# Second matrix of a sparse-attention and feed-forward kernel in two scaled halves, with a rewritten opening

## The chip, the cores and the metric

One core of one Trainium2 chip runs the whole program. The metric is device microseconds (us) of one execution. The engines are TensorE (PE, and PEld for its weight loads), VectorE (DVE), ScalarE (ACT), GpSimd (POOL) and SyncE (SP); SP and POOL also issue the DMA transfers that matter here, each on a queue of its own.

## The reference

Attention in blocks of 32 over 768 positions, then a feed-forward layer on its output. Only the parts that set the shapes are kept:

```python
B, H, S, D = 4, 8, 768, 64           # float32 q, k, v
mask = np.abs(blk_i - blk_j) <= 1
mask = mask | (blk_i == 0) | (blk_j == 0) | (blk_i == n_blocks - 1) | (blk_j == n_blocks - 1)
for qb in range(n_blocks):           # 24 blocks, 3 random ones for each
    for kb in sampled_blocks[qb]:
        mask[qb*32:(qb+1)*32, kb*32:(kb+1)*32] = True
scores = np.where(mask, q @ k.T / np.sqrt(D), -1e9)
attn = np.exp(scores - scores.max(-1, keepdims=True))
attn = attn / (attn.sum(-1, keepdims=True) + 1e-9)
x = (attn @ v).transpose(0, 2, 1, 3).reshape(3072, 512)
h = x @ w_in                          # 512 x 2048, float64
g = h * erf(np.maximum(h, 0) + np.log1p(np.exp(-np.abs(h))))
return g @ w_out                      # 2048 x 512, float64; out float32
```

## The kernel before, in words

**Numbers.** Products of the feed-forward layer and of the values run in f16: each factor is scaled by a power of two and split into a high half and a low half, and three of the four products of halves are added. The scale comes from a bound, the root of a sum of squares: `bound`, `whole_sum` and `pow2_scale` (L200) reduce the squares on each partition, add them over the partitions with one small matmul, and build the scale and its inverse with a few one-column steps on VectorE. The matrices arrive as 64-bit floats. For a pair of row blocks k (0 to 7) of `w_in` (i) or `w_out` (o) the program has five steps, named by a letter, the matrix and the pair: D decodes the raw words in three VectorE passes (`decode_pair`, L464), Q squares on ScalarE, H makes the high half on ScalarE, L the low half on VectorE; A and B (`sum_w`, `scale_w`) make the matrix' scale once all eight pairs are squared. Before, `w_out` has one scale, so no half of it exists before its eighth square.

**Attention.** A batch has three chunks of two tiles of four query blocks. A unit is a tile's scores for half of the heads (two pairs of heads): scores, maximum (`soft_max`), exponential on ScalarE (`soft_exp`), high and low half of the probabilities (`soft_low`), turning (`soft_turn`). Keys of the random blocks are copied by GpSimd. The values are split into four parts, `split_v` (L257), written to a table in DRAM (`vtab`), and gathered from there into `vb` by block number, the numbers being read from `samp` by `TENSOR_LOAD`. `values_of` multiplies, `norm` divides, `turn` splits and transposes the result for the feed-forward layer.

**Order.** Every instruction is kept in program order on its engine by the helper `InOrder`, so all rows of the trace carry its line, L59. The opening (L875 to L971) is written out by hand: loads, the bound of v, units 0 to 3, the decodes of `w_in` between them, its halves. Then a loop (L978) of 98 steps m runs over 96 groups of 256 rows of the feed-forward layer (4 batches, 3 chunks, 8 groups): the first product (`ff_first`) of group m, the gate of group m-1 (`ff_gate`, L726), the second product (`ff_second`, L735) of group m-2, and one attention unit in most steps. What is left of the two matrices' steps hangs in three tables of the loop, EARLY, AMID and LATE (L27 to L38), by step m: EARLY stands after `norm`, AMID after the gate's exponential, LATE after the turned probabilities.

```python
        if m < len(EARLY):
            work(EARLY[m])
        if m >= FF_LAG:
            for u in range(CT):
                ff_second(*groups[m - FF_LAG], u)
        if unit:
            soft_max(unit)
```

The accumulators `o` of a chunk take all eight groups, then `ff_store` (L748) multiplies by `iso` and writes. The raw words of the matrices are loaded by `load_weight`: 16 loads of 512 KB for each, on SP's or GpSimd's queue; those of `w_out` start as the decodes of `w_in` free their places (L472).

Of the kernel before, what the change touches and what calls it, by code (L numbers as in the profile page):

```python
# [18 lines left out]
P = 128  # L19
# [23 lines left out]
def sparse_attention_moe(ctx: ExitStack, tc: tile.TileContext, qT, kT, v, sampled, w_in, w_out, out):  # L43
# [140 lines left out]

    one = cp.tile([P, 1], F32, tag="one", name="one")
# [14 lines left out]
    def pow2_scale(whole, tag):  # L200
# [5 lines left out]
        s = st.tile([P, 1], F32, tag="s_" + tag[:2], name=f"s_{tag}", bufs=1)  # L206
        inv = st.tile([P, 1], F32, tag="i_" + tag[:2], name=f"i_{tag}", bufs=1)
# [43 lines left out]
    vns = {}  # L251

    def place_v(b, quad, half):

        place, tag, bufs = (mo, "xT", 3) if b == 0 and (quad, half) < (1, 1) else (at, "vn", 1)
        vn = place.tile([P, KT, 2, VW], F16, tag=tag, name=f"vn_{b}_{quad}_{half}", bufs=bufs)
        pool.memset(vn[:, :, :, D : D + 2], 1.0)  # L257
        vns[b, quad, half] = vn

    def split_v(b, quad, half):  # L260

        s = vscale[b][0]
# [9 lines left out]
        write = (whole_rows(b)[:, :, c : c + 2 * VW], vn.rearrange("p k h c -> p k (h c)"))  # L272
        if b == 0:
            sp.dma_start(*write)
        else:
            writes.append(write)
# [38 lines left out]
    kgs = {}  # L315
    POOL, SYNC = mybir.EngineType.Pool, mybir.EngineType.SP
# [13 lines left out]
    def gather(b, t):  # L330

        first, last = 1 + 4 * t, min(5 + 4 * t, NB - 1)
        blocks = block_numbers(first, last, POOL)
# [79 lines left out]
    wo16 = wo.rearrange("p n c -> p (n c)").bitcast(F16).rearrange("p (n c) -> p n c", c=1024)  # L413
    wsq = {"i": sums[:, P : P + 8], "o": sums[:, P + 8 : P + 16]}
# [49 lines left out]
    def decode_pair(key, k):  # L464
# [19 lines left out]
    def sum_w(key):  # L484
        wsums[key] = bound(wsq[key], f"w{key}", ALU.add)

    def scale_w(key):
        wscale[key] = pow2_scale(whole_sum(wsums.pop(key), f"w{key}"), f"w{key}")

# [245 lines left out]
    def ff_second(b, ch, fg, u):  # L735
        if fg == 0:
# [3 lines left out]
        for j in range(FG):  # L740
# [24 lines left out]

    results = []
# [118 lines left out]
    for n in range(3):  # L885
        place_v(0, *divmod(n, 2))
# [4 lines left out]
    for pr in range(HP):  # L891
        order_k(0, pr)
    place_v(0, 1, 1)
    order_q(0, 0)
    have_k.add(0)
    gathers(0)
# [15 lines left out]
    work("Di0")
    soft_low(units[0])
    work("Qi0")
    have_v.add(0)

# [157 lines left out]
```

## Time and profile before

| | |
|---|---|
| time, median of 3 runs | 838.31 us (838.24 to 840.38) |
| span of the profiled execution | 836.8 us |
| TensorE busy | 710.8 us, 85% of the span |
| VectorE busy | 554.4 us, 66% |
| ScalarE busy | 601.1 us, 72% |
| GpSimd busy | 123.7 us, 15% |
| DMA, mean | 157 GB/s |

The span is that of one execution taken by the hardware profiler; the page gives no other time for it, and it is set beside the median of the runs. Busy shares are averages over the span: an engine with 85% may be full in one stretch and starved in another. The stretch up to the first matmuls of the loop (87 us) and the first dozen steps of the loop are where the lines of the diff act; the gates of all later steps are touched as well.

### The profile page before, as it was taken

How to read it: one execution, taken by the hardware profiler on the slowest of the kernel's cores; microseconds unless marked ns; L12 is line 12 of the kernel's file. 1: busy time of each engine (PE TensorE's matmuls, PEld its weight loads, DVE VectorE, ACT ScalarE, POOL GpSimd, SP SyncE). 2: the span in 40 equal slices, each digit the busy share in tenths (PEclk: the TensorE clock that was granted, in tenths of full speed). 3: DMA queues.
4: the chain of work that ended last, by engine and by line, in shares of the span. 5: the costliest groups of instructions: out<-in, count | busy, mean ns of one | idle time of the engine just before them, and what ended most of it. 6: DMA issues, size and time to landing. Idle time of an engine off the chain costs nothing.

```text
span 836.8 us, 26712 instructions
## 1 busy us (share of the span) xinstructions
PE 710.8 (85%) x11100; PEld 504.8 (60%) x11100; DVE 554.4 (66%) x977; ACT 601.1 (72%) x999; POOL 123.7 (15%) x344
## 2 busy tenths in 40 slices
PE   1253637899897899899999899999999899999997
PEld 1252424566665667566777666667777576766664
DVE  3994796887764766766566676756677567654454
ACT  4654657987865766887768778868678678776774
POOL 5430111001222220100201231000111100000000
PEclk9775867989998999999999999999999999999999
DMA  8999953687899697661497886633576758211000
GB/s 325 297 257 318 243 120 90 164 207 164 172 212 209 178 205 198 186 131 45 136 216 178 210 198 192 167 79 83 117 167 166 190 103 188 53 33 40 1 27 26
DMA packets 199930, 131.61 MB, mean 157 GB/s; under 512 B 144000, under 2 KB 167168, under 8 KB 199808
## 3 DMA queue, kind: packets, MB, share of 16 engines
q1 hardware_dynamic: 196384, 118.10, 58.1%
q0 software_dynamic: 3424, 11.80, 4.3%
q8 instruction: 87, 1.43, 0.7%
q14 instruction: 35, 0.29, 0.1%
HBM read 83.88 MB, written 12.95 MB: 116 GB/s over the span
## 4 chain that ended last, share of the span: by engine, by line
PE 47%; DVE 15%; issue 12%; ACT 10%; DMA 10%; SPq 2%; POOL 2%; POOLq 1%; ACTq 0%
PE h L59 18%; PE o L59 18%; PE s_m L59 5%; DMA vb<-vtab 4%; PE po L59 3%; DVE g L59 2%; ACT pf_m L59 2%; DVE q L59 2%; DVE mx_m L59 2%; DMA vtab<-vn 2%; SPq L59 2%; ACT x L59 2%; DVE p_m L59 2%; POOL kg L59 2%; ACT q L59 2%
## 5 line engine op out<-in xcount | busy, mean ns | idle before, releaser
L59 PE MATMUL h<-xT,wi 128*128 128x256 f16 x2304 | 274.2, 276 | 14.9 <-ACT wi L59 7.5
L59 PE MATMUL o<-wo,g 128*128 128x512 f16 x1152 | 270.3, 385 | 7.9 <-DVE wo L59 4.0
L59 PEld LDWEIGHTS <-wi 128*128 128x128 f16 x2304 | 227.4, 99 | 65.5 <-ACT wi L59 8.8
L59 PEld LDWEIGHTS <-g 128*128 128x128 f16 x1152 | 110.3, 99 | 133.0 <-issue 14.8
L59 ACT ACTIVATE x<-x 128x512 f32<-128x512 f32 x288 | 181.5, 630 | 9.1
L59 POOL COPY kg<-kx 128x128 f32 x264 | 90.5, 394 | 286.2 <-PE s_m L59 183.6
L59 ACT ACTIVATE pf_m<-s_m,nb_m 128x256 f32<-128x256 f32 x160 | 62.7, 475 | 65.4 <-DVE nb_m L59 59.5
L59 DVE SCALAR_TENSOR_TENSOR q<-x,q 128x512 f32<-128x512 f32 x96 | 66.7, 695 | 61.4 <-ACT x L59 60.1
L59 ACT ACTIVATE x<-h,isg 128x512 f32<-128x512 f32 x96 | 65.2, 680 | 36.3 <-PE h L59 35.7
L59 PE MATMUL s_m<-kx,qm 128*64 128x64 f32 (+1 forms) x1280 | 75.0, 249 | 6.8 <-ACT pf_m L59 4.2
L59 ACT ACTIVATE q<-q 128x512 f32<-128x512 f32 x96 | 59.5, 620 | 29.6 <-DVE q L59 29.6
L59 DVE SCALAR_TENSOR_TENSOR q<-q,h 128x512 f32<-128x512 f32 x96 | 65.5, 682 | 22.6 <-ACT q L59 22.6
L59 DVE TENSOR_TENSOR p_m<-pf_m,p_m 128x1024 f16<-128x1024 f32 x40 | 49.3, 1232 | 32.3 <-ACT p_m L59 32.3
L59 DVE SCALAR_TENSOR_TENSOR g<-q,g 128x512 f16<-128x512 f32 x96 | 67.0, 698 | 3.3
L59 PE MATMUL po<-vb,pT_m 128*32 128x65 f16 (+1 forms) x3840 | 44.7, 201 | 25.7 <-DMA vb<-vtab 15.0
L59 PEld LDWEIGHTS s_m<-kx,qm 128*64 128x64 f32 x1280 | 59.7, 146 | 10.4 <-ACT pf_m L59 4.9
L59 ACT ACTIVATE q<-x 128x512 f32<-128x512 f32 x96 | 60.5, 630 | 3.1
L59 DVE TENSOR_REDUCE mx_m<-s_m 128x4 f32<-128x1024 f32 x40 | 48.8, 1219 | 20.2 <-PE s_m L59 20.2
L59 PEld LDWEIGHTS <-pT_m 128*32 128x32 f16 x3840 | 38.0, 97 | 36.8 <-DMA vb<-vtab 16.3
L59 PE MATMUL s_m<-kg,qm 128*64 128x96 f32 x640 | 46.9, 261 | 3.2 <-POOL kg L59 2.2
L59 DVE TENSOR_TENSOR x<-xf,x 128x512 f16<-128x512 f32 x24 | 16.9, 703 | 43.3 <-ACT x L59 43.3
L59 DVE TENSOR_SCALAR g<-q 128x512 f16<-128x512 f32 x96 | 41.3, 431 | 3.3
(115 smaller groups left out, 623.7 us busy)
## 6 DMA issues: line engine op xcount, KB each, us to landing
vb<-vtab SPq DMA_DIRECT2D x280, 65.0 KB, 2.9
vb<-vtab SPq DMA_DIRECT2D x32, 390.0 KB, 4.1
vraw<-in_v_dram SPq DMA_DIRECT2D x10, 768.0 KB, 5.1
vtab<-vn SPq DMA_DIRECT2D x16, 390.0 KB, 5.4
vb<-vtab SPq DMA_DIRECT2D x12, 520.0 KB, 5.0
qt<-in_qT_dram SPq DMA_DIRECT2D x20, 256.0 KB, 3.3
out_dram<-wo SPq DMA_DIRECT2D x20, 256.0 KB, 4.3
vb<-vtab SPq DMA_DIRECT2D x36, 130.0 KB, 3.0
```

Of the source, the lines that this page charges most:

```text
L59: done = call(*args, **kwargs)
```

## The change

Three things are done together.

1. `w_out` has two scales, one for pairs 0 to 3 (key p) and one for pairs 4 to 7 (key q), kept in a tile `levels`. The first chunk's second product uses both: its accumulators are closed after four groups, scaled by the inverse of p's scale into `partial`, opened again for the other four, and added at the end. A new step C (`level`) takes the smaller of the two scales for all later chunks, and a share for each half by which the gate (`ff_gate`) is multiplied: from a column of `levels` instead of a constant, in 88 of the 96 gates.
2. The opening loads v ahead of k and q, puts all four parts of v's halves in one place (`first_v`, in `wo`), writes them in two transfers instead of four, reads the first block numbers early, and copies the last two pairs of keys on GpSimd instead of VectorE. Raw blocks 0 to 5 of `w_in` are loaded by SP, the others by GpSimd, 8 to 15 behind gathers; raw blocks 0 to 7 of `w_out` are loaded by SP behind the eighth decode, behind the gathers of the values so far.
3. The opening and the tables are rewritten: four halves of `w_in` are made ahead of the loop, one decode of `w_out`; in the loop the high halves of `w_out` from pair 5 on stand in AMID of the step whose LATE has their low half (before: high in LATE of one step, low in AMID of the next).

```diff
-EARLY = ("", "", "Ao Bo Ho0 Lo0", "Hi5", "Hi6", "Hi7")
-AMID = ("Do3 Qo1 Qo2", "Do5", "", "Li5 Lo2", "Li6 Lo3", "Li7 Lo4", "Lo5", "Lo6", "Lo7")
+EARLY = ("Do1", "Ap Bp Ho0", "", "", "", "Aq", "Lo4")
+AMID = ("Qo0 Qo1 Do2", "Lo0 Do4", "Do5", "Ho2 Do6", "Ho3 Do7", "Hi7", "Ho5", "Ho6", "Ho7")
 LATE = (
-    "Qo3 Do4 Hi2 Li2 Qo4 Hi3 Li3",
-    "Qo5 Do6 Qo6 Do7 Qo7",
-    "Hi4 Ho1 Li4 Lo1 Ho2",
-    "Ho3",
-    "Ho4",
-    "Ho5",
-    "Ho6",
-    "Ho7",
+    "Qo2 Do3 Qo3",
+    "Ho1 Qo4 Lo1 Wo12 Wo13 Wo14 Wo15",
+    "Hi4 Qo5 Li4",
+    "Lo2 Hi5 Qo6 Li5",
+    "Lo3 Hi6 Qo7 Li6",
+    "Li7 Bq Cq Ho4",
+    "Lo5",
+    "Lo6",
+    "Lo7",
 )
...
-        copy = pool.tensor_copy if b else dve.tensor_copy if pr > 1 else act.copy
+        copy = pool.tensor_copy if b or pr > 1 else act.copy
...
         if b == 0:
-            sp.dma_start(*write)
+            if half == 1:
+                four = first_v[:, :, quad * 4 : quad * 4 + 4].rearrange("p k h c -> p k (h c)")
+                sp.dma_start(whole_rows(b)[:, :, quad * QW : quad * QW + QW], four)
...
+    first_v = wo[:, 11:, :].rearrange("p n c -> p (n c)").bitcast(F16)[:, : KT * H * VW]
...
-        freed = {4: (0, 1), 5: (2, 3), 6: (4, 5), 7: (6, 7)} if key == "i" else {2: (8, 9), 3: (10, 11)}
+        freed = {} if key == "i" else {2: (8, 9), 3: (10, 11)}
         for i in freed.get(k, ()):
-            load_weight(sp if key == "i" and k > 4 else pool, "o", i)
+            load_weight(pool, "o", i)
...
+        parts = wsq["i"] if key == "i" else wsq["o"][:, :4] if key == "p" else wsq["o"][:, 4:]
+        wsums[key] = bound(parts, f"w{key}", ALU.add)
...
+    def level(key):
+        (sp_, ip), (sq_, iq) = wscale["p"], wscale["q"]
+        least = levels[:, 4:5]
+        dve.tensor_tensor(least, sp_, sq_, ALU.min)
+        whole = levels[:, 5:6]
+        dve.tensor_tensor(whole, ip, iq, ALU.max)
+        wscale["o"] = (least, whole)
+        for c, n, inv in ((6, "p", ip), (7, "q", iq)):
+            shares[n] = levels[:, c : c + 1]
+            dve.tensor_scalar(shares[n], least, inv, 2.0**-H_SHIFT, ALU.mult, ALU.mult)
...
     def ff_gate(b, ch, fg):
-        scale = 2.0**-H_SHIFT
+        scale = 2.0**-H_SHIFT if (b, ch) == (0, 0) else shares["p" if fg < NGR // 2 else "q"]
         dve.scalar_tensor_tensor(hs, hs, -1.0, h, ALU.add, ALU.mult)
         dve.tensor_scalar(g[:, 0], hs, scale, None, ALU.mult)
...
     def ff_store(b, ch, fg, u):
+        early = (b, ch) == (0, 0)
+        if fg == NGR - 1 or (early and fg == NGR // 2 - 1):
+            key = "o" if not early else "p" if fg < NGR // 2 else "q"
...
+            ob = partial[0][:, u] if key == "p" else wo[:, NF + t % 2, :]
+            if key == "q":
+                dve.scalar_tensor_tensor(ob, outs[u], iso, partial[0][:, u], ALU.mult, ALU.add)
+            elif u == 0:
                 act.activation(ob, outs[u], AF.Copy, scale=iso)
             else:
                 dve.tensor_scalar(ob, outs[u], iso, None, ALU.mult)
...
+    for quad in range(2):
+        load_v(0, quad)
     for pr in range(HP):
         load_k(0, pr)
     load_q(0, 0)
-    for quad in range(2):
-        load_v(0, quad)
-    for i in range(4):
+    for i in range(6):
         load_weight(sp, "i", i)
-    load_q(0, 1)
-    load_q(0, 2)
...
-    work("Qi6 Di7 Qi7 Do0")
-    set_apart()
+    work("Qi6 Di7 Qi7")
+    for i in range(8):
+        load_weight(sp, "o", i)
...
-    work("Bi")
+    work("Bi Hi0")
     first_scale(0)
     values_of(seen(units[1]))
+    norm(*seen(units[1]))
     gathers(0)
-    for i in (12, 13, 14, 15):
-        load_weight(pool, "o", i)
-    norm(*seen(units[1]))
-    work("Hi0")
+    set_apart()
+    work("Li0 Hi1")
     turn(*seen(units[1]))
...
-    work("Li0 Hi1")
-    soft_turn(units[3])
     norm(*seen(units[2]))
-    work("Li1 Do1")
     values_of(seen(units[3]))
-    work("Qo0")
     norm(*seen(units[3]))
+    work("Li2 Hi3")
     turn(*seen(units[3]))
-    work("Do2")
+    work("Li3 Do0")
     gathers(0)
```

SP's queue at the start of the program, where `vb<-in_v_dram` and `vraw` are the two loads of v, `kr` those of k, `qt` of q, `wi` raw blocks, `vtab` the writes of v's halves and `vb<-vtab` gathers. Before:

```order
L59 DMA samp_85<-in_sampled_dram 128x144
L59 DMA kr_0_106<-in_kT_dram 128x768
L59 DMA qt_0_114<-in_qT_dram 128x4x128
L59 DMA vb<-in_v_dram 128x4x384
L59 DMA vraw_1_117<-in_v_dram 128x1536
L59 DMA wi<-in_w_in_dram 128x1024 x4
L59 DMA qt_1_123<-in_qT_dram 128x4x128
L59 DMA qt_2_125<-in_qT_dram 128x4x128
L320 TENSOR_LOAD samp
L59 DMA vtab_94<-vn_0_0_127 128x6x260
L59 DMA vtab_94<-vn_0_1_129 128x6x260
```

And with the change:

```order
L60 DMA samp_85<-in_sampled_dram 128x144
L60 DMA vb<-in_v_dram 128x4x384
L60 DMA vraw_1_108<-in_v_dram 128x1536
L60 DMA kr_0_110<-in_kT_dram 128x768
L60 DMA qt_0_118<-in_qT_dram 128x4x128
L60 DMA wi<-in_w_in_dram 128x1024 x6
L325 TENSOR_LOAD samp
L60 DMA vtab_95<-wo 128x6x520 x2
L60 DMA qt_1_254<-in_qT_dram 128x4x128
L60 DMA qt_2_256<-in_qT_dram 128x4x128
L60 DMA vb<-vtab_95 32x2x1040 x2
```

Both loads of v now stand ahead of the keys, two more weight loads stand ahead of the writes, the later q loads behind them, and two writes take the place of four.

VectorE at the end of the opening, where `rinv`, `xf` and `x` belong to `norm` and `turn`, `wi<-wi,s_wi` is a low half of `w_in`, and three passes from `wo` by `spare_k` back to `wo` are one decode of `w_out`. Before:

```order
L59 SCALAR_TENSOR_TENSOR wi<-wi,s_wi 128x2x512
L59 TENSOR_SCALAR spare_k<-wo 128x1024
L59 SCALAR_TENSOR_TENSOR spare_k<-wo,spare_k 128x1024
L59 SCALAR_TENSOR_TENSOR wo<-wo,spare_k 128x1024
L59 TENSOR_SCALAR rinv_1_1_1206<-po_1_1_1107 128x4
L59 RECIPROCAL rinv_1_1_1206<-rinv_1_1_1206 128x4
L59 TENSOR_TENSOR xf_1_1101<-po_1_1_1107,rinv_1_1_1206 128x256
L59 TENSOR_TENSOR x_0_1_1210<-xf_1_1101,x_0_1_1210 128x512
L59 TENSOR_SCALAR spare_k<-wo 128x1024
L59 SCALAR_TENSOR_TENSOR spare_k<-wo,spare_k 128x1024
L59 SCALAR_TENSOR_TENSOR wo<-wo,spare_k 128x1024
L59 TENSOR_REDUCE mx_m_2_0_1326<-s_m_2_0_1301 128x4
```

And with the change:

```order
L60 TENSOR_SCALAR rinv_1_1_1187<-po_1_1_1090 128x4
L60 TENSOR_TENSOR xf_1_1088<-po_1_1_1090,rinv_1_1_1187 128x256
L60 SCALAR_TENSOR_TENSOR wi<-wi,s_wi 128x2x512
L60 TENSOR_TENSOR x_0_1_1193<-xf_1_1088,x_0_1_1193 128x512
L60 SCALAR_TENSOR_TENSOR wi<-wi,s_wi 128x2x512
L60 TENSOR_SCALAR spare_k<-wo 128x1024
L60 SCALAR_TENSOR_TENSOR spare_k<-wo,spare_k 128x1024
L60 SCALAR_TENSOR_TENSOR wo<-wo,spare_k 128x1024
L60 TENSOR_SCALAR spare_k<-wo 128x1024
L60 SCALAR_TENSOR_TENSOR spare_k<-wo,spare_k 128x1024
L60 SCALAR_TENSOR_TENSOR wo<-wo,spare_k 128x1024
L60 TENSOR_REDUCE mx_m_2_0_1311<-s_m_2_0_1283 128x4
```

Before, the second decode stands ahead of the last values' division (`rinv_1_1`) and the third ahead of unit 4's maximum (`mx_m_2_0`). Now two low halves of `w_in` stand around `x`, then the first decode, the last work of the opening, and the second one, that of EARLY[0].

VectorE in m6, where `mx_f` and `nb_f` are the unit's maximum, `q_0_6` and `g` belong to the gate, `p_f` is the low half of its probabilities, `wo<-wo,...` is a low half of `w_out`, and `vn` the low halves of the next values. Before:

```order
L59 TENSOR_REDUCE mx_f_0_2623<-s_f_0_2599 128x1
L59 TENSOR_SCALAR nb_f_0_2625<-mx_f_0_2623 128x1
L59 SCALAR_TENSOR_TENSOR q_0_6_2478<-x_0_6_2474,q_0_6_2478 128x512
L59 SCALAR_TENSOR_TENSOR wo<-wo,s_wo 128x2x512
L59 TENSOR_TENSOR p_f_0_2630<-pf_f_0_2628,p_f_0_2630 128x768
L59 SCALAR_TENSOR_TENSOR vn_1_1_2641<-vraw_1_1964,s_v_2438,vn_1_1_2641 128x6x64 x2
```

And with the change:

```order
L60 SCALAR_TENSOR_TENSOR wo<-wo,levels 128x2x512
L60 TENSOR_REDUCE mx_f_0_2635<-s_f_0_2608 128x1
L60 TENSOR_SCALAR nb_f_0_2637<-mx_f_0_2635 128x1
L60 SCALAR_TENSOR_TENSOR q_0_6_2487<-x_0_6_2483,q_0_6_2487 128x512
L60 TENSOR_TENSOR p_f_0_2642<-pf_f_0_2640,p_f_0_2642 128x768
L60 SCALAR_TENSOR_TENSOR wo<-wo,levels 128x2x512
L60 SCALAR_TENSOR_TENSOR vn_1_1_2653<-vraw_1_1948,s_v_2447,vn_1_1_2653 128x6x64 x2
```

There is one low half more in this step (pair 4's, ahead of the maximum), and pair 5's now stands behind `p_f` instead of ahead of it.

## Rows read from the trace of the kernel before

**Rows 1.** The page: span, and busy time of the engines with share and instructions.

```profile
span 836.8 us, 26712 instructions
...
PE 710.8 (85%) x11100; PEld 504.8 (60%) x11100; DVE 554.4 (66%) x977; ACT 601.1 (72%) x999; POOL 123.7 (15%) x344
```

**Rows 2.** Table of stretches: stretch, length, busy PE, PEld, DVE, ACT, POOL, granted clock, DMA, GB/s.

```profile
16.80:60.00 43.20, 20.67 (x338) 18.40 (x338) 40.71 (x50) 27.73 (x48) 17.50 (x31) 0.76 0.98 290
60.00:87.24 27.24, 9.18 (x322) 6.93 (x323) 14.53 (x30) 12.10 (x17) 4.40 (x14) 0.62 0.98 296
87.24:134.50 47.26, 25.48 (x326) 17.00 (x326) 35.58 (x51) 30.08 (x51) 7.47 (x16) 0.72 0.56 145
134.50:175.05 40.55, 34.08 (x674) 24.30 (x673) 34.17 (x59) 36.64 (x59) 4.84 (x19) 0.91 0.75 184
87.24:91.60 4.36, 4.36 (x26) 3.06 (x27) 1.32 (x2) 0.00 (x0) 1.05 (x2) 0.62 0.87 207
176.30:203.73 27.43, 25.44 (x453) 18.24 (x451) 20.76 (x36) 21.35 (x34) 4.03 (x8) 1.00 0.83 180
```

**Rows 3.** Timeline, 57 to 130 us: start, duration, engine, work, [idle before it, releaser].

```profile
59.74 1.22 DVE L59 TENSOR_REDUCE mx_m<-s_m 128x4 f32<-128x1024 f32 x1
...
77.87 0.16 DVE L59 TENSOR_SCALAR rinv<-po 128x4 f32<-128x4 f32 x1 [9.32 <-PE po L59]
...
87.24 4.36 PE L59 MATMUL h<-xT,wi 128*128 128x256 f16 x24 [1.11 <-ACT xT L59]
```

**Rows 4.** Timeline of TensorE, 80 to 260 us.

```profile
125.64 0.59 PE L59 MATMUL whole_wo<-one,top_wo 128*128 128x1 f32 x2 [11.62 <-DVE top_wo L59]
...
128.54 0.59 PE L59 MATMUL o<-wo,g 128*128 128x512 f16 x1 [2.31 <-ACT wo L59]
...
176.30 2.78 PE L59 MATMUL h<-xT,wi 128*128 128x256 f16 x24
...
203.73 0.39 PE L59 MATMUL s_e<-kx,qm 128*64 128x96 f32 x4 [1.99 <-ACT pf_f L59]
```

**Rows 5.** Timeline, the start.

```profile
6.62 1.95 ACT L59 COPY kx<-kr 128x768 f32<-128x768 f32 x4 [4.58 <-DMA kr<-in_kT_dram]
...
11.19 0.86 DVE L59 COPY qm<-qt 64x512 f32<-64x512 f32 x2 [0.16 <-DMA qt<-in_qT_dram]
...
13.06 0.84 ACT L59 ACTIVATE vj<-vb 128x768 bf16<-128x768 f32 x1 [4.49 <-DMA vb<-in_v_dram]
...
16.83 0.16 DVE L59 TENSOR_REDUCE top_v<-vsq 128x1 f32<-128x4 f32 x1 [4.78 <-ACT vj L59]
```

**Rows 6.** Groups of VectorE by form: out<-in, count | busy us, mean ns | idle before.

```profile
L59 DVE SCALAR_TENSOR_TENSOR g<-q,g 128x512 f16<-128x512 f32 x96 | 67.0, 698 | 3.3
...
L59 DVE TENSOR_SCALAR g<-q 128x512 f16<-128x512 f32 x96 | 41.3, 431 | 3.3
...
L59 DVE SCALAR_TENSOR_TENSOR spare_k<-wo,spare_k 128x1024 int32<-128x1024 int32 x10 | 12.3, 1226 | 0.3
...
L59 DVE SCALAR_TENSOR_TENSOR wo<-wo,s_wo 128x1024 f16<-128x1024 f32 x8 | 10.2, 1280 | 1.7 <-ACT wo L59 1.7
L59 DVE TENSOR_SCALAR wo<-o,iso 128x512 f32<-128x512 f32 x12 | 9.0, 751 | 3.7 <-PE o L59 2.8
...
L59 DVE TENSOR_SCALAR spare_k<-wo 128x1024 int32<-128x1024 int32 x10 | 7.0, 701 | 0.1
```

**Rows 7.** Chain of waits, 0 to 100 us: start, duration, what.

```profile
24.96 12.14 DMA vtab<-vn
...
71.40 4.59 DMA vb<-vtab
```

**Rows 8.** DMA view, 34 to 76 us: queue, packets, MB, share of 16 engines.

```profile
q0 software_dynamic: 1728, 6.29, 48.6%
```

**Rows 9.** Chain that ended last, whole span, by line.

```profile
by line: PE h L59 18.4%; PE o L59 18.2%; issue 11.9%; PE s_m L59 4.8%; DMA vb<-vtab 3.8%; PE po L59 3.3%; DVE g L59 2.4%; ACT pf_m L59 2.3%; DVE q L59 2.2%; DVE mx_m L59 2.1%; DMA vtab<-vn 2.0%; SPq L59 2.0%; ACT x L59 2.0%; DVE p_m L59 1.8
```

**Rows 10.** DMA view, 0 to 130 us: GB/s in 40 slices of 3.25 us.

```profile
GB/s 23 285 388 418 413 384 404 388 335 252 134 249 371 300 325 276 276 168 204 189 358 310 241 327 406 340 216 189 310 222 183 339 226 102 85 0 233 170 0 0
```

More of the change, by code (lines that the diff above doesn't have):

```diff
@@ L332, in gather @@
         first, last = 1 + 4 * t, min(5 + 4 * t, NB - 1)
-        blocks = block_numbers(first, last, POOL)
+        blocks = first_numbers.pop() if first_numbers else block_numbers(first, last, POOL)
         for i in range(first, last):
@@ L484, in sum_w, with scale_of @@
     def sum_w(key):
-        wsums[key] = bound(wsq[key], f"w{key}", ALU.add)
+        parts = wsq["i"] if key == "i" else wsq["o"][:, :4] if key == "p" else wsq["o"][:, 4:]
+        wsums[key] = bound(parts, f"w{key}", ALU.add)
     def scale_w(key):
         wscale[key] = pow2_scale(whole_sum(wsums.pop(key), f"w{key}"), f"w{key}")
+    def scale_of(key, k):
+        return wscale[key if key == "i" else "p" if k < 4 else "q"][0]
     def halves(key, k):
@@ L495, in split_hi @@
         w32, hi16, _ = halves(key, k)
-        act.activation(hi16, w32, AF.Copy, scale=wscale[key][0])
+        act.activation(hi16, w32, AF.Copy, scale=scale_of(key, k))
     def split_lo(key, k):
         w32, hi16, lo16 = halves(key, k)
-        dve.scalar_tensor_tensor(lo16, w32, wscale[key][0], hi16, ALU.mult, ALU.subtract)
-    steps_of = {"D": decode_pair, "Q": square_pair, "A": sum_w, "B": scale_w, "H": split_hi, "L": split_lo}
+        dve.scalar_tensor_tensor(lo16, w32, scale_of(key, k), hi16, ALU.mult, ALU.subtract)
+    shares = {}
+    def level(key):
[8 more added lines that the diff above has]
+            dve.tensor_scalar(shares[n], least, inv, 2.0**-H_SHIFT, ALU.mult, ALU.mult)
+    steps_of = {
+        "D": decode_pair,
+        "Q": square_pair,
+        "A": sum_w,
+        "B": scale_w,
+        "H": split_hi,
+        "L": split_lo,
+        "C": level,
+        "W": lambda key, k: load_weight(pool, key, k),
+    }
     def work(steps):
@@ L735, in ff_second @@
     def ff_second(b, ch, fg, u):
-        if fg == 0:
+        turns = (0, NGR // 2) if (b, ch) == (0, 0) else (0,)
+        starts = [n * FG for n in turns]
+        stops = [n - 1 for n in starts[1:]] + [NF - 1]
+        if fg in turns:
             outs[u] = ps_o.tile([P, DM], F32, tag="o", name=f"o_{b}_{ch}_{fg}_{u}")
@@ L757, in ff_store @@
                 dve.tensor_scalar(ob, outs[u], iso, None, ALU.mult)
+            if key == "p":
+                return
             r = b * S
@@ L890, in sparse_attention_moe @@
     dve.tensor_scalar(unity, column, pidx, None, ALU.is_equal)
[L891 to L896, printed above, removed]
+    first_numbers.append(block_numbers(1, 5, POOL))
     numbers[0] = block_numbers(1, 5, SYNC)
     early.append((0, 1))
-    for i in range(4, 10):
-        load_weight(pool, "i", i)
     for quad in range(2):
@@ L904, in sparse_attention_moe @@
     scale_v(0)
+    order_k(0, 0)
+    split_v(0, 0, 0)
+    order_k(0, 1)
+    order_k(0, 2)
+    order_k(0, 3)
+    split_v(0, 0, 1)
+    for i in (6, 7):
+        load_weight(pool, "i", i)
+    split_v(0, 1, 0)
+    order_q(0, 0)
+    split_v(0, 1, 1)
+    load_q(0, 1)
+    load_q(0, 2)
+    have_k.add(0)
+    have_v.add(0)
+    gathers(0)
+    for i in range(8, 12):
+        load_weight(pool, "i", i)
+    work("Di0")
     scores(units[0])
-    split_v(0, 0, 0)
-    split_v(0, 0, 1)
+    work("Qi0 Di1")
     soft_max(units[0])
-    split_v(0, 1, 0)
-    split_v(0, 1, 1)
     soft_exp(units[0])
[L912 to L915, printed above, removed]
+    work("Qi1 Di2")
     scores(units[1])
@@ L919, in sparse_attention_moe @@
     gathers(0)
-    for i in range(10, 16):
+    for i in range(12, 16):
         load_weight(pool, "i", i)
+    soft_low(units[0])
     soft_turn(units[0])
-    work("Di1")
+    work("Qi2 Di3")
     soft_max(units[1])
@@ L926, in sparse_attention_moe @@
     order_q(0, 1)
-    work("Qi1 Di2 Qi2 Di3 Qi3")
+    work("Qi3 Di4")
     soft_low(units[1])
+    scores(units[2])
     soft_turn(units[1])
-    scores(units[2])
-    work("Di4 Qi4 Di5")
+    work("Qi4 Di5")
     soft_max(units[2])
```

47 lines of the change are left out of this document (26 added, 21 removed).

## The prediction

> **What bounds the kernel now.** I read four views in this order. The page gives the share of each engine: TensorE is busy for 85% of the span, VectorE for 66%, ScalarE for 72% [rows 1]. An average says little here, so the table of stretches comes next: up to 60 us VectorE works almost without a hole (40.71 of 43.20 us), from 60 to 175 us it has holes, and TensorE falls behind in the whole stretch to 134.5 us [rows 2]. Two timelines then show the stalls that this change is about: the second tile's values wait for gathered rows (VectorE, which needs them next, waits 9.32 us), and TensorE waits 11.62 us ahead of the common scale of the second matrix [rows 3, 4]. From 176.30 us on TensorE runs without a gap that matters until 203.73 us (25.44 of 27.43 us busy, granted clock 1.00) [rows 2, 4]. So time is to be won only before 175 us, and what is won there must still be there when TensorE fills up.
>
> I call a pass over one half of the second matrix' pairs "half p" (pairs 0 to 3) and "half q" (4 to 7), and m0, m1, ... the steps of the main loop; m0's first matmul is at 87.24 us [rows 3].
>
> **The ledger.** VectorE ends last in most of this stretch, and up to the reduction of the loop's m6, which ends at the edge of a stretch in the table (175.05 us), it does the same work before and after. So I count: start, work, idle time. Before, it starts with the bound of v at 16.83 us [rows 5]; to 175.05 it is busy for 40.71 + 14.53 + 35.58 + 34.17 = 125.0 us of 158.2 and idle for 33.2: 2.5, 12.7, 11.7 and 6.4 by stretch [rows 2].
>
> *Start.* Four key loads and q stood ahead of v. Now v is first: its first load lands about when the first key load did (6.62 us, plus up to 1 us as it is twice as large) and no longer at 13.06; the squares took from there to 16.83, 3.77 us [rows 5]. Now they end at 11.3 to 12.4; I take 11.8, 5.0 us earlier.
>
> *Work added.* A second scale (a reduction and four steps of about 0.16 us, as the reduction in rows 5), four such steps for the least common level, and the eviction of half p's sum for one tile at 0.75 us [rows 6] with its 0.16 us factor: 2.5 us. The copy of q, 0.86 us [rows 5], moves behind the start. Together 3.4 us. The two key copies go from VectorE to GpSimd, where the gathers wait for ScalarE's copy of the second pair anyway: nothing; without that cover, their own copy time once, ahead of the first scores.
>
> *Gathers.* The two larger writes are issued after eight halves: the last was issued at 24.96 us [rows 7], now 5 us earlier, about 20. That write took 12.14 us and the last gather landed at 71.40 + 4.59 = 75.99 [rows 7], 38.9 us after the write. In that stretch GpSimd's queue moved 6.29 MB, twelve loads of 512 KB, at 48.6% of 42 us, so 1.70 us of all engines each [rows 8]. The change leaves four of the twelve there (the last four of the first matrix): 38.9 - 8 x 1.70 = 25.3 us. The write lands between 32 us (12.14 after its issue) and 39 (the third rival); I take 33, since its queue holds two more weight loads. The last gather then lands at 58. It is needed when unit 3 has been turned, at about 68 (below), so the 9.32 us wait is gone, with 10 us of cover. The eight raw loads of the second matrix that follow on SP's queue are needed 18 us later and have the queues to themselves.
>
> *Idle time to m0.* Of 2.5 + 12.7 us, 9.3 go: 5.9 stay. But a hole needs work to fill it: the second and third decode of the second matrix, three passes of 0.70, 1.23 and about 1.23 us each, so 6.3 us [rows 6], stood there and now stand behind m0's matmuls. I add 6: 12 us in all. The first matmul of m0 follows. Behind the last half of v at 20 us stand eight first-matrix decodes (25.3), four reductions of 1.22 us [rows 3] with a 0.16 us step each (5.5), three low halves of probabilities (3.6, an estimate: each like a decode's second pass) and 2.5 us of holes: unit 3's reduction ends at 56.9 instead of 61.0 [rows 3]. From there to 87.24 were 26.2 us; less 9.3 for the gathers, and 2.6 more for two added low halves of the first matrix (1.28 each, as those of the second [rows 6]): m0 begins at about 76, 11 us earlier.
>
> *Idle time m0 to m2.* The 11.7 us of holes here are where the decodes now fall: I leave 1.5. Half p needs only four decodes. From m0's first matmul to the first of the second layer, 128.54 [rows 4], were 41.3 us, with five decodes and the 11.62 us wait; now there are three decodes and, I take it, 2 us of that wait: 41.3 - 6.3 - 9.6 = 25.4, so about 101. These 27 us are not a gain: the other four decodes and all later halves come after it.
>
> *Idle time m3 to m6.* 6.4 us before. m4 now needs the high and low half of first-matrix pair 5, the last work of VectorE in m3, and m6 that of pair 7. By VectorE's order in m3 I estimate that TensorE waits 10 us in m4. [...] VectorE then lacks values and scores for 4 us. I take 11.
>
> The sum: start 11.8, work 125.0 + 3.4, idle 12 + 1.5 + 11 = 24.5, so m6's reduction is done at 164.7 instead of 175.05: 10.3 us earlier.
>
> *What is given back.* From here TensorE needs a low half of the second matrix in every step. Before, it was made directly behind the score's scale and the first gate product; now it stands behind the probabilities' low half and thus behind ScalarE's copy, while the high half has moved ahead. A low half takes 1.28 us [rows 6]; with part of the copy's wait I count 1.8 us a step, in the three steps (m6 to m8) in which TensorE had no gap: 5.5 us. Bounds: nothing, if TensorE's queue covers it, and all 10.3, if it meets every step to m9.
>
> *The gate's scale.* In 88 of 96 gates two VectorE instructions take a scalar per partition instead of a constant. Nearest rows: a three-operand pass of 1024 columns costs 1.226 us with a constant and 1.280 with a scalar of this kind, 0.054 more. For the two-operand one, 0.431 us, the only such row with a scalar per partition reads PSUM and takes 0.751: bounds +0.054 and +0.32 [rows 6]. I take the lower, because the other row differs in its source too. [...] 88 x 2 x 0.054 = 9.5 us of VectorE. Of the gate's 67.0 + 41.3 = 108.3 us [rows 6], the chain that ended last holds 2.4% of 836.8 = 20.1 [rows 9], 18.6%: 1.8 us. At the upper bound 88 x (0.054 + 0.32) = 32.9, of which 6.1.
>
> **Sum.** -10.3 + 5.5 + 1.8 = -3.0 us on a profiled span of 836.8, so 833.8. The median of the runs shown, 838.31, is 1.5 above that span, for what lies around it; on it the forecast is **835.3 us**. A measurement of this kernel can tell about 0.3%, 2.5 us, from no change, so the forecast lies just beyond that line.
>
> **Rivals.**
> - *The low halves cost TensorE nothing.* Speaking for it: two matmul groups stand ahead of them in each step. Then -10.3 + 1.8: 829.8.
> [...]
> - *Slower: the writes stand behind the weights.* Six loads are on SP's queue ahead of the two writes. If they still hold it when the writes are issued, the write lands 6 x 1.25 us later than its 12.14 (512 KB at the 418 GB/s of the best slice [rows 10]): 39. If gathers then take the old 38.9 us, the last lands at 78, where it is needed at 68: m0 comes 10 us later than in my sum, and with nothing won before it the total is -3.0 + 10 = +7; some of the 10 us is taken from holes that m1 and m2 have anyway, so +5, 843. It decides from a last gather at 68 on. Against it: the first slices moved 285 to 418 GB/s [rows 10], by which the 6.6 MB that I count ahead of the writes are done by about 20 us. [...]
> - *The scalar takes the gate's faster rate away.* +6.1 instead of +1.8: 839.6.
>
> **How the numbers follow.** Forecast as worked out, 832 to 838: 0.50, of which 0.33 lies beyond the 0.3% line. The first rival 0.12 (faster). All given back 0.16 (0.12 same, 0.04 slower). Writes behind weights 0.17 (slower). The gate's rate 0.05 (0.02 same, 0.03 slower). Faster 0.45, same 0.31, slower 0.24. The range leaves out the end of the first rival and of the third: 829 to 843.
>
> **What would show it.** Right: v's squares end near 12 us; the last gather lands before 65 and no matmul of the second tile waits for it; m0 at 76 and the first second-layer matmul near 101; waits of 1 to 3 us ahead of second-layer matmuls in m6 to m8. Wrong: a gather wait ahead of m0; gates of 0.75 us; TensorE's gap in m4 or m6 much over 10 us; a difference that arises after 220 us.

## The result

| | before | changed |
|---|---|---|
| median | 839.35 us (838.24 to 840.73, 4 runs) | 854.13 us (852.91 to 856.58, 4 runs) |
| ratio, 95% interval | | 1.0147 (1.0109 to 1.0185) |
| span of the profiled execution | 836.8 us | 852.9 us |

The change makes the kernel 1.5% slower by the ratio of the runs (the quotient of the two medians is 1.0176, within its interval); 835.3 us was forecast, with a range of 829 to 843. On a second chip the same pair came out at 1.0127 (1.0095 to 1.0159). The page of the changed kernel, span and busy time, against [rows 1]:

```profile
span 852.9 us, 26719 instructions
...
PE 718.6 (84%) x11102; PEld 511.7 (60%) x11102; DVE 566.2 (66%) x986; ACT 600.7 (70%) x999; POOL 138.2 (16%) x341
```

TensorE makes two matmuls more and is busy for 7.8 us longer, VectorE for 11.8; the span grows by 16.1, so about half of the loss is idle time of TensorE, and part of the rest is matmuls that ran at a lower granted clock behind a wait (m6's first product below, behind 9.25 us of waiting, takes 5.28 us at a granted clock of 0.50, against 2.78 at 1.00 [rows 2, 4]). Its table of stretches, cut where the new program has the places of [rows 2] (start of VectorE's work on v, 60 us, m0, m3, end of m6's reduction; columns as there):

```profile
11.45:60.00 48.55, 20.39 (x338) 18.52 (x338) 39.98 (x49) 28.54 (x50) 29.73 (x49) 0.89 1.00 304
60.00:83.45 23.45, 9.60 (x322) 7.64 (x323) 12.34 (x28) 13.74 (x19) 0.46 (x2) 0.52 0.86 273
83.45:120.96 37.51, 25.20 (x326) 18.54 (x326) 32.42 (x46) 24.92 (x44) 13.99 (x20) 0.75 0.78 226
120.96:177.60 56.64, 36.61 (x674) 25.43 (x673) 44.77 (x81) 40.33 (x66) 6.18 (x20) 0.79 0.60 135
```

VectorE is busy for 129.5 us of these 166.2 and idle for 8.6, 11.1, 5.1 and 11.9: 36.6 us. The timeline of VectorE in the opening, with the idle time before each in brackets (to [rows 3, 5]):

```profile
11.45 0.16 DVE L60 TENSOR_REDUCE top_v<-vsq 128x1 f32<-128x4 f32 x1 [2.74 <-ACT vj L60]
...
27.97 1.22 DVE L60 TENSOR_REDUCE mx_m<-s_m 128x4 f32<-128x1024 f32 x1 [1.70 <-PE s_m L60]
...
50.83 0.69 DVE L60 TENSOR_SCALAR spare_k<-wo 128x1024 int32<-128x1024 int32 x1 [3.59 <-DMA wo<-in_w_in_dram]
...
77.23 0.16 DVE L60 TENSOR_SCALAR rinv<-po 128x4 f32<-128x4 f32 x1 [3.87 <-PE po L60]
...
80.99 0.69 DVE L60 TENSOR_TENSOR x<-xf,x 128x512 f16<-128x512 f32 x1 [1.73 <-ACT x L60]
```

v is split early, as meant, and no wait for gathered rows is left. But a decode waits 3.59 us for its raw words, and behind 60 us VectorE waits for TensorE and ScalarE in turn. The timeline of TensorE from m0 to m9 (to [rows 4]):

```profile
83.45 5.17 PE L60 MATMUL h<-xT,wi 128*128 128x256 f16 x24 [1.11 <-ACT xT L60]
...
102.02 0.59 PE L60 MATMUL whole_wp<-one,top_wp 128*128 128x1 f32 x2 [6.26 <-DVE top_wp L60]
...
111.93 0.38 PE L60 MATMUL s_m<-kg,qm 128*64 128x96 f32 x2 [3.37 <-POOL kg L60]
...
135.43 0.61 PE L60 MATMUL h<-xT,wi 128*128 128x256 f16 x2 [5.52 <-ACT wi L60]
138.74 3.59 PE L60 MATMUL h<-xT,wi 128*128 128x256 f16 x16 [2.69 <-DVE wi L60]
...
158.06 0.38 PE L60 MATMUL whole_wq<-one,top_wq 128*128 128x1 f32 x2 [1.80 <-DVE top_wq L60]
...
167.92 5.28 PE L60 MATMUL h<-xT,wi 128*128 128x256 f16 x24 [9.25 <-DVE m_wq L60]
...
193.17 3.88 PE L60 MATMUL o<-wo,g 128*128 128x512 f16 x11 [2.35 <-DVE wo L60]
```

The second layer starts early (its first scale at 102 instead of 125.64 us), but m4 stands still for 8.2 us, m6 for 9.25. The starts of the first product by step, read from the timelines of the first chip's two kernels:

| first product of | m0 | m4 | m6 | m7 | m12 | m36 | m68 | last matmul ends |
|---|---|---|---|---|---|---|---|---|
| before | 87.2 | 142.8 | 162.0 | 176.3 | 215.6 | 414.1 | 650.7 | 832.4 |
| changed | 83.5 | 129.1 | 167.9 | 179.2 | 220.2 | 422.3 | 665.0 | 848.1 |

A lead of 13.7 us at m4 is lost by m6, where the changed kernel is 5.9 us behind; and of the 15.7 us at the end 11.1 arise **behind m12**, where both programs issue the same instructions in the same order, gates apart.

### The profile page after: what moved, and what is told of

It is laid out like the page before. It is cut to its first block, busy times and chain, and to the rows that moved or that the text cites. A ratio compares the mean times of both kernels' runs of the same rounds, so it can differ in the third digit from the quotient of the medians.

```text
span 852.9 us, 26719 instructions
## 1 busy us (share of the span) xinstructions
PE 718.6 (84%) x11102; PEld 511.7 (60%) x11102; DVE 566.2 (66%) x986; ACT 600.7 (70%) x999; POOL 138.2 (16%) x341
## 4 chain that ended last, share of the span: by engine, by line
PE 46%; issue 16%; DVE 13%; DMA 9%; ACT 7%; POOL 5%; SPq 2%; POOLq 1%; ACTq 0%; DVEq 0%
PE h L60 18%; PE o L60 17%; PE s_m L60 5%; POOL kg L60 4%; PE po L60 4%; DVE mx_m L60 2%; DVE q L60 2%; DVE g L60 2%; SPq L60 2%; DMA pT_m<-p_m 2%; ACT pf_m L60 2%; DMA vtab<-vn 2%; DMA wo<-in_w_in_dram 1%; DVE p_m L60 1%; ACT x L60 1%
## 5 line engine op out<-in xcount | busy, mean ns | idle before, releaser
L60 POOL COPY kg<-kx 128x128 f32 x264 | 102.2, 436 | 269.7 <-PE s_m L60 168.7
L60 PE MATMUL s_m<-kx,qm 128*64 128x64 f32 (+1 forms) x1280 | 79.5, 256 | 24.0 <-ACT pf_m L60 8.5
L60 PEld LDWEIGHTS s_m<-kx,qm 128*64 128x64 f32 x1280 | 63.7, 152 | 27.7 <-ACT pf_m L60 9.3
L60 DVE SCALAR_TENSOR_TENSOR g<-q,levels,g 128x512 f16<-128x512 f32 x88 | 66.1, 751 | 3.1
L60 PE MATMUL s_m<-kg,qm 128*64 128x96 f32 x640 | 52.3, 268 | 14.7 <-POOL kg L60 13.5
L60 PEld LDWEIGHTS s_m<-kg,qm 128*64 128x64 f32 x640 | 39.9, 153 | 18.2 <-POOL kg L60 16.9
```

The costliest lines, as they stand in the source:

```text
L60: done = call(*args, **kwargs)
```

## The experiments

The experiments ran on other chips, each beside runs of the kernel before on its chip; so ratios are compared, and ratios from different chips only with their intervals.

**Gate.** In e1 the changed kernel gets its constant back, in e4 the kernel before gets a scalar:

```diff
-        scale = 2.0**-H_SHIFT if (b, ch) == (0, 0) else shares["p" if fg < NGR // 2 else "q"]
+        scale = 2.0**-H_SHIFT
```

> The changed kernel with one edit: all 96 gates multiply by the constant again (it leaves out the shares of the two halves). Theory A (the gate's scalar is on the path): 88 gates lose 0.053 + 0.06 us on VectorE, 9.9 us in all, and the delay of the changed kernel grows from about +4.6 us at m12 to +14.7 at m51; if that growth is the scalar, this run comes to 844 to 846 us, and the growth is gone. Rival B (of the 9.9 us only the chain's share, some 2 us, counts; the growth comes from transfers that collide): 851 to 853 us, with the growth still there.

```diff
+    pair = cp.tile([P, 2], F32, tag="one", name="one")
+    share = pair[:, 1:2]
+    pool.memset(share, 2.0**-H_SHIFT)
...
-        scale = 2.0**-H_SHIFT
+        scale = 2.0**-H_SHIFT if (b, ch) == (0, 0) else share
```

> The kernel before with one edit: in 88 of 96 gates the constant is replaced by the same value in a column of a tile. Theory A (the scalar is on the path): +8 to +10 us, 847 to 849. Rival B (only the share of the chain that ended last, 18.6% of 9.9 us): +2 us, 840 to 842.

e1: 1.0091 (1.0056 to 1.0125), 3 to 5 us under the changed kernel's two ratios, with intervals that overlap; the delay behind m12 stayed (from m12's first product to the last matmul 627 us, 627.9 in the changed kernel). e4: 1.0019 (0.9994 to 1.0045), 848.87 against 846.71 us. By e4, whose runs of before were made on the same chip, rival B holds: the scalar is worth some 2 us, and at most 4 by the interval. e1 by itself lies between its two theories on time, and has rival B's growth. The groups of VectorE by form in e4 give the scalar's price, against 698 and 431 ns in [rows 6]:

```profile
L59 DVE SCALAR_TENSOR_TENSOR g<-q,one,g 128x512 f16<-128x512 f32 x88 | 67.1, 762 | 3.2
...
L59 DVE TENSOR_SCALAR g<-q,one 128x512 f16<-128x512 f32 x88 | 43.0, 489 | 3.1
```

**Halves of the first matrix.** e2 gives pairs 5 to 7 their old places:

```diff
-EARLY = ("Do1", "Ap Bp Ho0", "", "", "", "Aq", "Lo4")
+EARLY = ("Do1", "Ap Bp Ho0", "", "Hi5", "Hi6", "Hi7 Aq", "Lo4")
-AMID = (..., "Ho2 Do6", "Ho3 Do7", "Hi7", ...)
+AMID = (..., "Li5 Ho2 Do6", "Li6 Ho3 Do7", "Li7", ...)
...
-    "Lo2 Hi5 Qo6 Li5",
-    "Lo3 Hi6 Qo7 Li6",
-    "Li7 Bq Cq Ho4",
+    "Lo2 Qo6",
+    "Lo3 Qo7",
+    "Bq Cq Ho4",
```

> The changed kernel with one edit: high and low halves of pairs 5, 6 and 7 of the first matrix stand where they stood before the change (high in EARLY, low in AMID of m3, m4, m5). Theory A: the waits ahead of the first product in m4 (5.5 + 2.7 us) and m6 (9.3 us) come from their place behind the turned probabilities; they shrink to 2 to 4 us each, and the run comes to 843 to 848 us. Rival B: VectorE has the same work ahead of the same matmuls, so the wait moves to the second products or to the units, and the run stays at 851 to 855 us.

1.0049 (1.0014 to 1.0084): 0.8 to 1.0% off the changed kernel's ratios. m4's waits fell to 1.05 and 0.93 us, but m6's stayed at 7.02. VectorE and TensorE of e2 around it:

```profile
156.42 1.28 DVE L60 SCALAR_TENSOR_TENSOR wi<-wi,s_wi 128x1024 f16<-128x1024 f32 x1
...
161.15 0.15 DVE L60 TENSOR_SCALAR m_wq<-whole_wq 128x1 f32<-128x1 f32 x1
```

```profile
153.73 0.38 PE L60 MATMUL whole_wq<-one,top_wq 128*128 128x1 f32 x2 [0.40 <-DVE top_wq L60]
...
161.35 5.28 PE L60 MATMUL h<-xT,wi 128*128 128x256 f16 x24 [7.02 <-DVE m_wq L60]
```

Pair 7 is done at 157.7 us, and m6 still waits until `m_wq` has been read at 161.3. The code says why: `whole_sum` takes its tile from the three accumulators of the first product (`ps_h`, tag "h"). The sum for half q sits in one of them from 153.7 us until VectorE comes to B, which the change put into LATE. So e5 and e6 read it earlier, alone and with e2:

```diff
-AMID = (..., "Hi7", "Ho5", "Ho6", "Ho7")
+AMID = (..., "Bq Cq Hi7", "Ho5", "Ho6", "Ho7")
-    "Li7 Bq Cq Ho4",
+    "Li7 Ho4",
```

> The changed kernel with one edit: the second half's scale is read (B and C of q) at the head of AMID of m5 instead of behind the low half of pair 7 in LATE. Theory A: the first product of m6 waits for two things that end together at 167.7 to 167.9 us, the low half of pair 7 and the reading of the sum, which stands in one of the three accumulators of the first product; with one of them gone m6 starts its first six matmuls some 6 us earlier but waits for pair 7 in the middle, and at most 1 to 2 us are won in all. Rival B: only the accumulator holds m6; then its 24 matmuls are done 6 us earlier and the run is 5 to 7 us faster than the changed kernel.

> Both edits together: the halves of pairs 5 to 7 in their old places (as the second experiment) and the scale read at the head of AMID of m5. Theory A: nothing holds m6 any longer; its first product starts some 5 us earlier than with the halves alone, the wait of 7.0 us there falls under 2.5, and the run is 10 to 13 us faster than the changed kernel, near the kernel before (within 0.5%). Rival B: VectorE is the limit, and the wait moves to the second products of m6 to m9: no more than 2 us better than with the halves alone.

e5: 1.0084 (1.0054 to 1.0113) beside the changed kernel's 1.0127, 3.6 us less, which lies between the two forecasts (the intervals overlap). Its TensorE in m6:

```profile
161.40 1.44 PE L60 MATMUL h<-xT,wi 128*128 128x256 f16 x6 [2.29 <-DVE m_wq L60]
...
168.30 3.60 PE L60 MATMUL h<-xT,wi 128*128 128x256 f16 x16 [3.54 <-DVE wi L60]
```

The trace is theory A's: six matmuls start early, the rest stands still for pair 7. In m6 two things ended last together. e6: 1.0046 (1.001 to 1.0082), no better than e2. Its m6:

```profile
157.39 1.86 PE L60 MATMUL h<-xT,wi 128*128 128x256 f16 x8 [2.29 <-DVE m_wq L60]
...
168.84 4.85 PE L60 MATMUL o<-wo,g 128*128 128x512 f16 x11 [4.15 <-DVE wo L60]
```

The first product is 4 us earlier and the gain is spent on the low half of pair 4, 4.15 us late for the second: rival B.

**Other parts of the schedule.** e3 puts the two key copies back on VectorE (`dve.tensor_copy if pr > 1`), e7 is e6 with the constant gate, e8 is e7 with the low halves in their old order, e9 is e8 with the second tile turned first:

```diff
-EARLY = (..., "Hi7 Aq", "Lo4")
+EARLY = (..., "Hi7 Aq")
-AMID = (..., "Bq Cq Li7", "Ho5", "Ho6", "Ho7")
+AMID = (..., "Bq Cq Li7 Ho4", "Lo5", "Lo6", "Lo7")
-    "Ho4",
-    "Lo5",
-    "Lo6",
-    "Lo7",
+    "Lo4 Ho5",
+    "Ho6",
+    "Ho7",
...
-    work("Li2 Hi3")
     turn(*seen(units[3]))
-    work("Li3 Do0")
+    work("Li2 Hi3 Li3 Do0")
```

> The changed kernel with one edit: the last two key copies of the opening are made by VectorE again. Theory A: on GpSimd they hold up its random-key copies (which ran 16.4 to 25.2 us instead of 14.2 to 17.1) and with them unit 0's scores; without them the first reduction comes 3 to 5 us earlier than 27.97 us, but m0 moves by less than 2 us, since decodes fill the time, and the run stays within 2 us of the changed kernel. Rival B: the whole opening moves with it: m0 4 us earlier and the run 3 to 5 us faster.

e3: 1.0094 (1.006 to 1.0129). Neither theory: the first reduction came at 27.05 us, where e1 with the copies on GpSimd had it at 27.18 on the same chip, and m0 moved by 0.2 us. These copies cost nothing that can be told, as the forecast had it.

> The previous experiment (halves of pairs 5 to 7 in their old places, scale read early) with the constant in all gates again (the shares are left out). Theory A: the delay that builds up in the attention steps from m14 to m51 is the gate's scalar; 3 to 5 us faster than the previous one, ratio to the kernel before 0.999 to 1.002. Rival B: the scalar costs 1.8 us: ratio 1.002 to 1.004.

> As the kernel beside it with the constant gate, and the low halves of pairs 4 to 7 of the second matrix in their old order (low half in AMID, the next high half behind it in LATE). Theory A: the low halves behind the turned probabilities cost TensorE some 5 us in m6 to m9 (waits of 2.4 us ahead of a second product); these waits go, and the run is 4 to 6 us faster than the kernel beside it, ratio 0.993 to 0.997. Rival B: VectorE only changes the order of the same work and the gain is under 1.5 us.

> As the kernel with the low halves in old order, and in the opening the second tile is turned ahead of the low half of pair 2 and the high half of pair 3 of the first matrix. Theory A: these two halves stand on the chain to m0 (low half, high half, then the tile's copy on ScalarE); m0's first product comes 2 us earlier, and the run 0 to 2 us. Rival B: m0 starts when it did, since something else ends last there.

e7: 1.0034 (1.0001 to 1.0066); e8: 1.0043 (1.0012 to 1.0073); e9: 1.0028 (0.9996 to 1.006), its m0 at 82.3 instead of 83.5 us. By the runs nothing happened. By the steps much did: e8 starts m7 at 166.2 us and m12 at 207.0, 9 to 10 us ahead of the kernel before in its first profile. That lead was gone at the end. This points to something behind m12 that is not in the order of the instructions.

**The place of the tiles.** To see what the chips do behind m12, both kernels ran again beside each other:

> The changed kernel unchanged, beside the experiments on one chip: 1.2 to 1.8% slower than the kernel before, with m0 earlier and the first product of m6 later than in the kernel before on the same chip. If the loss were a matter of the first chip, it would fall under 0.8% here.

> The kernel before unchanged, for its steps on the same chip as the experiments: within 0.5% of the runs of before beside it. Theory: on this chip its later steps are delayed against the first profile too, so that part of the growth after m12 that the experiments show belongs to the chip; rival: its steps are where they were, and all of that growth belongs to the change.

1.0127 for the changed kernel, and the kernel before at 842.0 us in its one run. From m12's first product to the last matmul it takes 619.0 us here and 616.8 on the first chip, the changed kernel 630.8 and 627.9, e8 633.6. So the growth of 11 to 12 us belongs to the change and not to a chip. What differs there is where tiles lie. `levels` is 32 bytes per partition wide and is made ahead of the two weight tiles and of every large tile behind them, so all of these move by 32 (`qm` and `vb` lie ahead of it and stay). Addresses of the source of the probabilities' transposes in the compiled programs:

```
kernel                       address   beyond that of before
before, e4, f1, f2, f4       193536    0
changed, e1 to e3, e5 to e9, f3   193568    32
g1 / g2 / g3                 193568 / 193600 / 193664    32 / 64 / 128
```

f1 makes `levels` behind the large tiles; f2 is e8 with that, f4 is f2 with the gates' shares; f3 moves the tiles of the kernel before:

```diff
-    levels = cp.tile([P, 8], F32, tag="levels", name="levels")
+    levels = st.tile([P, 8], F32, tag="levels", name="levels", bufs=1)
```

```diff
-    one = cp.tile([P, 1], F32, tag="one", name="one")
+    wide_one = cp.tile([P, 16], F32, tag="one", name="one")
+    one = wide_one[:, 0:1]
...
+        if tag == "wo":
+            s, inv = wide_one[:, 8:9], wide_one[:, 9:10]
```

> The changed kernel with one edit: the 32-byte tile of the levels is placed behind all large tiles, so that these lie at multiples of 64 bytes again. Theory A (the shift costs): the transposes by DMA fall from 5.2 to below 4.9 us, the growth after m12 falls from some 11 us to 2 to 5, and the run is 6 to 9 us faster than the changed kernel, ratio to the kernel before 1.002 to 1.006. Rival B (the place is indifferent; the growth comes from the phase in which the steps arrive): ratio 1.011 to 1.016 as before.

> The version with the old places of all halves, the early reading of the scale and the constant gate (it leaves out the shares), now without the shift. Theory A: the lead of some 10 us at m12 is kept, ratio 0.987 to 0.992. Rival B: the lead is lost as in the same version with the shift, ratio 1.001 to 1.007.

> The kernel before with one edit: one tile ahead of the large ones is 32 bytes wider (and takes the second matrix' scale and its inverse), which shifts all large tiles as the change does. Theory A: 6 to 10 us slower than the kernel before, ratio 1.007 to 1.012, growing from m12 to m68. Rival B: no difference, ratio 0.998 to 1.002.

> The version with the old places of all halves and the early reading of the scale, with two scales and the gates' shares kept, without the shift. Theory A: 2 to 4 us behind the one with the constant gate, ratio 0.990 to 0.996: faster than the kernel before. Rival B: ratio 1.002 to 1.008.

| run | ratio (95% interval) | m12 to last matmul |
|---|---|---|
| f1, the change without the shift | 1.0006 (0.9978 to 1.0033) | 619.8 us |
| f2, e8 without the shift | 0.9910 (0.9878 to 0.9941) | 616.6 us |
| f3, before with the shift | 1.0108 (1.0073 to 1.0144) | 625.2 us |
| f4, as f2 with two scales and shares | 0.9921 (0.9888 to 0.9954) | 621.7 us |

Theory A in all four, f1 by more than it said. The shift alone costs 1.1%, and taking it away gives the changed kernel 1.2 to 1.4% back. The ratios carry this. The last column is of one execution each, f2's being its fastest, 4.6 us under its median, and it differs by chip: e4, without the shift, takes 623.6 us where before takes 846.71. f4 is faster than both kernels: 837.36 us beside 844.28. Its m6 and m7 in TensorE's timeline, with the halves in their old places, start 10.5 and 12.0 us earlier than in the changed kernel's first profile:

```profile
157.43 1.60 PE L59 MATMUL h<-xT,wi 128*128 128x256 f16 x8 [2.29 <-DVE m_wq L59]
...
167.16 2.78 PE L59 MATMUL h<-xT,wi 128*128 128x256 f16 x24
```

TensorE's and VectorE's busy time hardly moved with the shift: TensorE is busy for 715.9 us in f3, 710.8 and 714.9 in the two profiles of before, VectorE for 554.3, 554.4 and 554.5. What did move is the time that SP takes to issue a transpose of the probabilities by DMA. The view of that tile from 205 to 655 us (count: duration in ns, smallest, median, largest, first and last start), one row each for before, changed, f1 and f3:

```profile
L59 SPq DMA_TRANSPOSE pT_m<-p_m x26: 1317/1840/3762, 226.2 to 653.1; - x26
```

```profile
L60 SPq DMA_TRANSPOSE pT_m<-p_m x25: 1517/2725/4249, 231.0 to 649.4; - x25
```

```profile
L60 SPq DMA_TRANSPOSE pT_m<-p_m x25: 1581/2097/3861, 230.1 to 640.7; - x25
```

```profile
L59 SPq DMA_TRANSPOSE pT_m<-p_m x25: 1326/2674/4377, 229.8 to 647.0; - x25
```

The gathers stand behind it on SP's queue, and the values wait for both: from 205 to 655 us TensorE's idle time ahead of the values' product has 5.7 us that a gather ended and 3.9 that such a transpose ended before, 6.7 and 6.2 in the changed kernel. Which tile's place counts was the last question: source, target, or all others.

```diff
 # g1: 32 bytes ahead of the source, 32 behind it
+    pool.memset(at.tile([P, 8], F32, tag="pad3", name="pad3", bufs=1), 0.0)
...
+    pool.memset(at.tile([P, 8], F32, tag="pad4", name="pad4", bufs=1), 0.0)
```

g2 has the same two pads around the target, g3 a pad ahead of everything, of the target, of the tiles behind it, and of the source. All three keep two matrices' scales in the tile of ones, to make room; that was not run alone. Tiles behind a pad move too: in g1 `g`, `xT`, `q` and `x`, by 64 bytes, in g2 also the source, by 64, in g3 every tile from the weights on.

> The kernel before, with only the probabilities' halves (the source of the transposes by DMA) moved 32 bytes off a multiple of 64. Theory A (the transposes read or write rows worse off such an address): if the source decides, the issue of a transpose takes 2.6 to 2.9 us instead of 2.0 and the run is 0.6 to 1.2% slower; if the target decides, no difference (0.998 to 1.002) and the next run shows it. Rival B (the other tiles pay: copies, loads, weights): no difference here nor in the next.

> The kernel before, with only the turned probabilities (the target of the transposes) moved 32 bytes off. Theory A: one of this and the run beside it is 0.6 to 1.2% slower, or both share it, 0.3 to 0.8% each. Rival B: ratio 0.998 to 1.002.

> The kernel before, with the weights, keys, gathered keys, raw and split values and exponentials moved 32 bytes off, and the source and the target of the probabilities' transposes left where they were. Theory A: under 0.4% slower, transposes at 2.0 to 2.2 us. Rival B: 0.7 to 1.2% slower with the transposes as before.

1.0123 (1.0056 to 1.0189), 1.0108 (1.003 to 1.0187) and 1.0117 (1.0058 to 1.0175): each pays in full. Neither theory survives as written: g2 and g3 were meant to spare the source, and moved it by 64 and 128 bytes. g3's transposes, whose source and target lie at multiples of 64:

```profile
L59 SPq DMA_TRANSPOSE pT_m<-p_m x25: 1319/2859/4454, 234.2 to 651.3; - x25
```

So it was not enough that both lie at multiples of 64. In none of the three is the source at 193536, while it is in all five kernels of the first line above; the medians of those five are 1840 to 2178 ns, those of the others 2428 to 2874.

The transfers themselves separate the two groups more sharply. The same view for the transposes of `p_f`, from issue to landing, before and in g1:

```profile
DMA to landing us min/median/max: 3.2/3.3/4.2
```

```profile
DMA to landing us min/median/max: 3.7/3.7/5.2
```

In the six profiles with the source at 193536 the quickest takes 3.2 us, in the fourteen others 3.6 to 3.8; for `p_m` it is 3.6 to 3.8 and 4.2 to 4.4. The transposes of `x`, whose source and target moved by 32 bytes in f3 too, take 3.1 to 3.5 at the quickest in both groups: not every transfer became slower. In g1 the target of `p_f`'s transposes stays where it was. So, as far as these runs can tell, what lengthens these transfers goes with their source. g1 also says that the weights, the keys and the turned probabilities need not move for the kernel to pay in full.

Why the place of the source counts is not shown: 193536 is its only place in these runs without the longer transfers, and other tiles moved along in g1 to g3. That half a microsecond on each such transfer adds up to the 10 us of the kernel is not shown either.

## Why the prediction was wrong

**Right.** The start: VectorE's bound of v at 11.45 us, 11.8 forecast. The gathers: no wait for them ahead of m0; the rival of the writes behind the weights did not happen. Work added: 129.5 us against 128.4. Idle time in m3 to m6: 11.9 against 11, with m4's wait 8.2 against 10; that this sum came out is partly luck, since TensorE stood still for 9.25 us more in m6, which the forecast did not have, while VectorE was mostly busy. No run of before shows the 4 us for which the forecast lets VectorE lack values and scores behind m4's wait; in the changed kernel it waits there 3.11 us for the values' product and 1.07 us for the scores, behind 16 matmuls that took 3.59 us at a granted clock of 0.50. The gate's scalar near its lower bound: 0.064 and 0.058 us an instruction (e4), 1 to 2 us of time by e4, by e6 to e7 and by f4 to f2, 1.8 forecast.

**Wrong, the first step: "I add 6: 12 us in all".** VectorE was idle for 19.7 us up to m0, not 12, and m0 came at 83.45, not 76. The step took the 9.32 us wait for gathers [rows 3] out and named too little of what is late next: raw words (3.59 us), and behind 60 us the row of turning, multiplying and dividing that passes between TensorE and ScalarE at a granted clock of 0.52. From m0 to m2 it was 5.1 us instead of 1.5, as GpSimd's keys came late (TensorE waits 3.37 us for them); the first product of the second layer came at 117.7 us, not 101. Together 11.3 of the 12.9 us by which m6's reduction (177.6) missed 164.7. "*What is given back*" was smaller than its term: 2 us between m6's reduction and m12, not 5.5.

**Wrong, in the place of its wait.** The forecast named pair 7 as what m6 needs, gave it no time, and did not see that the second half's sum would hold an accumulator; e2 and e5 show that both end there together and that removing either alone leaves a wait, e6 that without both the wait moves to the second product.

**Wrong, the missing term.** The ledger counts "start, work, idle time", and has nothing for the new tile itself, though the forecast's own list of signs has "a difference that arises after 220 us". The tile moved nearly every large tile by 32 bytes, and the kernel paid some 10 us behind m12 (627.9 against 616.8 us), which f1 takes back. Without it the change is worth +0.5 us (1.0006, interval -1.9 to +2.8) where -3.0 was forecast: no difference that can be told. So the schedule's terms lost the gain, and the term that was missing made a loss of it. The ledger does not close: with m6's reduction 12.9 us later and 3.5 us less given back it would put the change at +6.4 us, not +0.5. Part of the shift's price may lie ahead of m12 (f1 starts m12 at 218.7 us, f3, the kernel before with the shift on the same chip, at 219.1); the rest stays open.

## What to carry to other kernels

Where a delay grows although both programs issue the same instructions there, compare where the tiles lie as well as the schedule: here a 32-byte tile ahead of the large ones cost more than the whole change was to win, and with the tile behind them that loss was gone (f1). A lead at some step is worth nothing until the last step has it, so read the starts of all steps, not the stall that a change removes. And when two things end together (an accumulator and a half), taking one away shows little of the gain; taking both away shows only what the next wait leaves (e6).

## What the runs showed of the hardware

A shift of nearly all large tiles by 32 bytes costs this kernel 1.1% (f3), with TensorE busy for 715.9 us against 710.8 and 714.9 before, VectorE for 554.3 against 554.4 and 554.5. The median issue of a transpose of `p_m` by DMA is 1.84 to 2.18 us in the five kernels with its source at 193536 and 2.43 to 2.87 in the others, and its quickest transfer takes 3.6 to 3.8 us and 4.2 to 4.4. The gate's VectorE pass of 512 columns with a scalar per partition, reading SBUF, takes 0.489 us (e4) against 0.431 with a constant, far from the 0.751 of the nearest row, from PSUM [rows 6].
